# Block diagonal by small DMAs, column-tiled state weights, merged row sums and a new order of steps in a one-core kernel

## The chip, the cores and the metric

One core of one Trainium2 chip. The metric is device microseconds of one execution. Most executions of a kernel agree within a few tenths of a per cent here, but some are slower: a run is called slow when it is over 1.5% above the fastest of the same kernel. Verdicts use the other runs, called fast, and each kernel is compared with runs of the kernel before made in the same rounds on the same chip. A ratio below is the mean time of a kernel's fast runs over the mean of the fast runs of the kernel before of the same rounds, so it is not quite the ratio of the medians that are quoted. Intervals are 95%.

TensorE is PE in the profile, its weight loads are PEld, VectorE is DVE, ScalarE is ACT, GpSimd is POOL. Times in the views are microseconds from the start of the span. The span is about 1.8 us shorter than the run's time.

## The reference, cut to what matters

```python
# x: 8 batches x 8 heads x 512 x 64, state: 8 x 8 x 32 x 64
a  = softmax(scale * x @ state.T)        # 512 x 32 a head
xread = a @ state
a2 = softmax(scale * state @ x.T)        # 32 x 512
sread = a2 @ x
y = concat([xread, sread], axis=2)       # 8 x 8 x 544 x 64
# heads put side by side: z is 8 x 544 x 512
wq, wk = z @ w_q, z @ w_k                # 544 x 64
W = wq @ wk.T / 8
out = maximum(W @ z, 0) @ w_out          # 8 x 544 x 512, float32
```

Of the kernel before, what the change touches and what calls it, by code (L numbers as in the profile page):

```python
# [8 lines left out]
FP = mybir.dt.float32  # L9
# [4 lines left out]


ORDER = """
zst.0.p ix1.0.p stc.0.v xc1.0.a fill.1.t stt.0.c ste.0.v stbd.0.p stf.0.a xc0.0.p xc3.0.v ix2.0.p
fill.7.t xT0.0.t xc2.0.v xTe0.0.a fill.1.t xT1.0.t is.0.p stc.1.v fill.1.t stt.1.c xTe1.0.v stbd.2.p
fill.1.t pt0.0.t stf.1.v fill.1.t pt1.0.t exp0.0.a ste.1.v iwo.0.p exp1.0.a rs0.0.v fill.4.t
sums.0.t ix3.0.p rinv0.0.v wc.0.a fill.1.t xT0.1.t rs1.0.v fill.1.t srd.0.r xTe0.1.v A0.0.p fill.1.t  # L20
xT1.1.t fill.1.t sw.0.r xTe1.1.a rinv1.0.v fill.1.t pt0.1.t srn.0.v A1.0.p at0.0.t srT.0.t exp0.1.a
pt1.1.t srTe.0.v sbd.0.p swe.0.a xT0.2.t rs0.1.v at1.0.t exp1.1.a xT1.2.t xTe0.2.v stbd.1.p ate.0.a
xTe1.2.v fill.1.t stt.2.c stt.3.c rs1.1.v ste.2.a pt0.2.t stbd.6.p stf.3.v exp0.2.a fill.1.t wq.0.c
ste.3.v wks.0.c ix4.0.p stf.2.a wk.0.t rs0.2.v sw.3.r pt1.2.t wke.0.v swe.3.a stbd.3.p sw.1.r
rinv.1.v exp1.2.a g.0.t sw.2.r ge.0.v stbd.5.p swe.1.a rs1.2.v sums.2.t v.0.c wqe.0.a rinv.2.v
xT1.3.c swe.2.a A.1.p ve.0.v xT0.3.c xTe1.3.a srd.2.r xTe0.3.v mix0.0.r mix1.0.r mxe0.0.v sums.1.t
mxe1.0.a A.2.p srd.1.r at.1.t pt1.3.t srn.1.v ate.1.a fin0.0.t srn.2.v ix5.0.p xT1.4.t exp1.3.a
srT.1.t xT0.4.t xTe1.4.v srTe.1.a fin1.0.t sbd.1.p xTe0.4.a rs1.3.v pt1.4.t wq.1.c sbd.2.p exp1.4.a
wks.1.c wqe.1.v pt0.4.t oe0.0.a srT.2.t wk.1.t rs1.4.v at.2.t ix6.0.p fin2.0.t ate.2.v wke.1.a
os0.0.s exp0.4.a stbd.7.p g.1.t srTe.2.v fin3.0.t ge.1.v rs0.4.v sums.4.t stbd.4.p oe1.0.a srd.4.r  # L30
rinv.4.v v.1.c srn.4.v wq.2.c A.4.p ve.1.a os1.0.s srT.4.c wks.2.c wk.2.t srTe.4.a mixs.1.r wke.2.v
mix1.1.r wqe.2.a mix0.1.r mse.1.v xT1.5.t mxe0.1.a ix7.0.p at.4.t xTe1.5.v g.2.t xT0.5.t mxe1.1.a
ge.2.v sbd.4.p pt1.5.t xTe0.5.v v.2.c exp1.5.a fin2.1.c ve.2.v pt0.5.c rs1.5.v mixs.2.r mix1.2.r
exp0.5.a ate.4.v xT1.6.c mse.2.a sums.5.c fin3.1.c xTe1.6.a rs0.5.v rinv.5.v xT0.6.c mxe1.2.a
oe1.1.v A.5.p pt1.6.c wq.4.c srd.5.r exp1.6.a mix0.2.r srn.5.v os1.1.s fin0.1.c mxe0.2.a rs1.6.v
sbd.5.p xT0.7.c xTe0.6.v fin0.2.c xTe0.7.a wqe.4.v pt0.6.c srT.5.c at.5.c exp0.6.a xT1.7.c ate.5.v
srTe.5.a fin1.2.c xTe1.7.a rs0.6.v wq.5.c rinv.6.v wks.5.c wk.5.c wqe.5.a pt1.7.c A.6.p wke.5.v
wks.4.c sums.6.c exp1.7.a srd.6.r g.5.t oe0.2.a rs1.7.v wk.4.t pt0.3.t fin1.1.t srn.6.v exp0.3.a
os0.2.s wke.4.v sbd.6.p at.6.t oe0.1.a rs0.3.v srT.6.t g.4.t fin2.2.t ate.6.v os0.1.s fin3.2.t
ge.5.v ge.4.v srTe.6.v v.5.c oe1.2.a rinv.3.v wq.6.c ve.5.v A.3.p wks.6.c wk.6.c v.4.c os1.2.s  # L40
wke.6.a wqe.6.v mix1.5.r ve.4.a mixs.5.r mix0.5.r mxe1.5.v sums.3.t mxe0.5.a g.6.t srd.3.r mixs.4.r
ge.6.v mix0.4.r mse.5.a mix1.4.r srn.3.v mxe0.4.a v.6.c mse.4.v sbd.3.p srT.3.c pt0.7.c srTe.3.v
at.3.c mxe1.4.a ve.6.v fin2.5.c ate.3.v exp0.7.a fin3.5.c rs0.7.v wq.3.c oe1.5.a wks.3.c fin0.4.c
rinv.7.v A.7.p wqe.3.a os1.5.s mix0.6.r mixs.6.r wk.3.t mse.6.a fin1.4.t wke.3.a mxe0.6.a g.3.t
oe0.4.v at.7.t sums.7.t ate.7.a srd.7.r mix1.6.r srn.7.v os0.4.s fin2.4.c mxe1.6.v sbd.7.p srT.7.c
fin3.4.c srTe.7.a ge.3.v fin2.6.c oe1.4.v v.3.c fin3.6.c ve.3.v os1.4.s fin0.5.c oe1.6.a fin1.5.c
os1.6.s mix1.3.r oe0.5.v mixs.3.r wq.7.c mxe1.3.a wks.7.c wk.7.c mixs.0.r mse.3.v mix0.3.r os0.5.s
mse.0.a wke.7.v fin0.6.c wqe.7.a mxe0.3.a g.7.c fin1.6.c ge.7.a fin0.3.c oe0.6.v fin1.3.c os0.6.s
v.7.c oe0.3.a fin2.3.c ve.7.a fin3.3.c os0.3.s mix0.7.r oe1.3.a mixs.7.r fs.3.t mxe0.7.v mse.7.a
os1.3.s mix1.7.r fse.3.v fs.7.t mxe1.7.a fse.7.v fix1.7.t fix2.7.t oc1.7.a fix0.7.t oc2.7.a fix3.7.t  # L50
oc0.7.a oc3.7.b
"""


# [1 line left out]
def kernel(  # L56
# [9 lines left out]
    nc = tc.nc  # L66
    ctx.enter_context(tc.manual_schedule())

    B, H, S, D = x.shape
    NS = state.shape[2]  # L70
# [6 lines left out]
    NP = H // 2  # L77
# [13 lines left out]
    st_bf = const.tile([128, B, 2, D], BF, name="st_bf")  # L91
    stT = const.tile([128, B, 2, H, NS], BF, name="stT")
    stbd = const.tile([128, B, 2, NP, D], BF, name="stbd")
    w_f = const.tile([128, NP, 2, DH], FP, name="w_f")
    w_qk = const.tile([128, NP, 2, DH], BF, name="w_qk")
    w_o = const.tile([128, KC, DM], BF, name="w_o")
    sw = const.tile([128, B, 2, 2, DH], BF, name="sw")
# [35 lines left out]
    nc.vector.memset(mask, 0.0)  # L133
    for q in range(NP):
        nc.vector.memset(mask[NS * q : NS * q + NS, q : q + 1], 1.0)

    L = [dict() for _ in range(B)]
    G = {}
# [59 lines left out]
        copy(e, st_bf[:, b0:b1], st_f[:, b0:b1])  # L198

    def zeros(n, b, e):  # L200
        nc.gpsimd.memset(stT.bitcast(FP), 0.0)

    def w_cast(n, b, e):
        if e == "p":
# [36 lines left out]
    def sw_mm(n, p, e):  # L241
        ps = psA.tile([128, 2, 512], FP, name="sw_ps", tag="psA")
        for bb in range(2):
            for q in range(NP):
                for r in range(2):
                    nc.tensor.matmul(
                        out=ps[NS * q : NS * q + NS, r, 2 * DH * bb : 2 * DH * bb + 2 * DH],
                        lhsT=stT[64 * r : 64 * r + 64, 2 * p + bb, r, NP * r + q, :],
                        rhs=w_qk[64 * r : 64 * r + 64, q, 0:2, :],
                        start=True,  # L250
                        stop=True,
                    )
        G["sw", p] = ps
# [363 lines left out]
    def fs_ev(n, b, e):  # L617
# [5 lines left out]
    STEP = {  # L623
        "ix": load, "iwo": load, "is": load, "wc": w_cast, "xc": x_cast, "stc": st_cast,
        "zst": zeros, "stt": st_tr, "ste": st_ev, "stf": st_ev,
        "stbd": stbd_blk, "fill": fill, "fix": fin_mm, "os": fin_st,
        "sw": sw_mm, "swe": sw_ev, "xT": xT_mm, "xTe": xT_ev, "xs": x_dT, "as": a_dT, "pt": pt_mm, "exp": pt_exp,
        "rs": rs, "rinv": rv, "A": nrm, "at": at_mm, "ate": at_ev,
        "srd": srd, "sums": sums, "srn": srn, "sbd": sbd, "srT": srT_mm, "srTe": srT_ev,
# [5 lines left out]
    for tok in ORDER.split():  # L635
        n, b, e = tok.split(".")
# [31 lines left out]
```

## The kernel before: the parts that the change and the argument touch

The kernel is written as a list of steps, `name.batch.engine`. Every engine runs its own steps in the order of this list, so the list is the schedule. For PE the last letter is the form of a matmul: `t` is one 128x128 tile, `c` is two column halves (two instructions), `r` is a form of its own (row or 32-column tiles). `ix` and `iwo` are loads of x and of the output weights, `stbd` the block diagonal of the state, `sw` the state times the projection weights, `rs` row sums, `fill` matmuls on zeros that only keep PE running.

```python
ORDER = """
zst.0.p ix1.0.p stc.0.v xc1.0.a fill.1.t stt.0.c ste.0.v stbd.0.p stf.0.a xc0.0.p xc3.0.v ix2.0.p
fill.7.t xT0.0.t xc2.0.v xTe0.0.a fill.1.t xT1.0.t is.0.p ... iwo.0.p exp1.0.a rs0.0.v fill.4.t
sums.0.t ix3.0.p ...
"""                                        # cut; some 400 steps

def load(n, b, e):
    if n == "iwo":
        nc.gpsimd.dma_start(out=w_o, in_=moe_w_out.rearrange("(k p) e -> p k e", p=128))
    elif n == "is":
        nc.gpsimd.dma_start(out=st_bf[:, 3:B], in_=st_src[:, 6 : 2 * B])
    else:
        b = int(n[2:])
        nc.gpsimd.dma_start(out=x_bf[b], in_=xsrc(b, 0, H))       # 512 KB of x, cast on the way

def zeros(n, b, e):
    nc.gpsimd.memset(stT.bitcast(FP), 0.0)

def stbd_blk(n, b, e):                     # one batch: two multiplications on GpSimd
    for r in range(2):
        nc.gpsimd.tensor_tensor(out=stbd[:, b, r], in0=st_bf[:, b, r : r + 1, :].to_broadcast((128, NP, D)),
            in1=mask[:, :, None].to_broadcast((128, NP, D)), op=ALU.mult)

def sw_mm(n, p, e):                        # 16 matmuls for two batches
    for bb in range(2):
        for q in range(NP):
            for r in range(2):
                nc.tensor.matmul(
                    out=ps[NS * q : NS * q + NS, r, 2 * DH * bb : 2 * DH * bb + 2 * DH],
                    lhsT=stT[64 * r : 64 * r + 64, 2 * p + bb, r, NP * r + q, :],
                    rhs=w_qk[64 * r : 64 * r + 64, q, 0:2, :], start=True, stop=True)

for tok in ORDER.split():
    n, b, e = tok.split(".")
    STEP["".join(i for i in n if not i.isdigit())](n, int(b), e)
```

The softmax here doesn't subtract the row's maximum and nothing guards it: scores larger than these inputs give would overflow.

## Time and profile before

| | before |
|---|---|
| time, median of the runs beside the changed kernel | 88.25 us (87.77 to 88.51, 4 runs) |
| span of the profiled run | 87.0 us |
| PE busy | 80.8 us, 93% |
| DVE, ACT, POOL busy | 52.4, 55.9, 45.1 us |
| PE idle inside the span (87.0 - 80.8) | 6.2 us |
| instructions of PE and PEld in the trace | 1572 + 1579 |

The table is read from the top: one engine is busy 93% of the span, no other above 64%, so the length of PE's stream sets the time. The lines behind it stand in the prediction. The last row also belongs here, and the prediction did not look at it.

One more view of the kernel before belongs here: the posts of x on GpSimd, from its timeline (start, duration, engine, line, operation). This one is batch 4.

```profile
17.71 0.94 POOL L183 DMA_DIRECT2D x_bf<-in_x_dram  x1
```

### The profile page before, as it was taken

The page shows a single profiled execution, that of the slowest core. Times are in us where ns is not written, and L with a number is a line of the kernel's source. Part 1 is how long each engine was busy: PE and PEld are TensorE (multiplying, and loading weights), DVE is VectorE, ACT ScalarE, POOL GpSimd, SP SyncE. Part 2 cuts the span into 40 slices and gives each one's busy share as a digit, 9 for nine tenths or more (in the row PEclk, how much of TensorE's full clock was granted, in tenths as well). Part 3 has the DMA queues.
Part 4 walks back from the last instruction along what each step waited for, and adds up shares of the span by engine and source line. Part 5 has one row for each costly group of instructions (what it writes and reads, how often), then busy time and mean ns, then how long its engine had stood idle before and what let it go on. Part 6 is the DMA issues. An engine that isn't in the chain of part 4 may idle for free.

```text
span 87.0 us, 3553 instructions
## 1 busy us (share of the span) xinstructions
PE 80.8 (93%) x1572; PEld 53.4 (61%) x1579; DVE 52.4 (60%) x111; ACT 55.9 (64%) x83; POOL 45.1 (52%) x58
## 2 busy tenths in 40 slices
PE   4999999999999999999999999999999999999910
PEld 1326666878777778777689747866755565544400
DVE  2125793997956875897856957891688264056010
ACT  1541637999898858778797838967930592665530
POOL 7999948999999969408507735327150000000000
PEclk9999999999999999999999999999999999999996
DMA  0899999999609999995600464201461663566782
GB/s 12 292 312 187 202 191 198 195 165 147 96 0 121 143 128 277 322 169 72 241 8 4 171 281 175 115 8 53 188 243 45 275 281 136 213 269 277 294 314 80
DMA packets 15119, 15.00 MB, mean 172 GB/s; under 512 B 3712, under 2 KB 12672, under 8 KB 15104
## 3 DMA queue, kind: packets, MB, share of 16 engines
q0 software_dynamic: 9104, 4.36, 39.7%
q1 hardware_dynamic: 4880, 8.98, 28.0%
q10 hardware_dynamic: 1120, 1.44, 4.6%
q8 instruction: 12, 0.20, 0.9%
q14 instruction: 3, 0.02, 0.1%
HBM read 10.22 MB, written 8.91 MB: 220 GB/s over the span
## 4 chain that ended last, share of the span: by engine, by line
PE 90%; ACT 4%; issue 1%; DVE 1%
PE fin_ps L161 20%; PE fin_ps L163 12%; PE fill_ps L155 6%; PE xT_ps L174 5%; PE mix_ps L541 5%; PE warm_ps L132 4%; PE srd_ps L369 3%; PE xT_ps L170 3%; PE at_ps L174 3%; PE v_ps L505 3%; PE pt_ps L163 2%; PE g_ps L163 2%; PE fins_ps L163 2%; PE wq_ps L433 2%; PE v_ps L514 2%; PE wk_ps L163 2%
## 5 line engine op out<-in xcount | busy, mean ns | idle before, releaser
L346 POOL TENSOR_TENSOR A<-E,rinv 128x1024 bf16<-128x1024 bf16 (+1 forms) x9 | 15.4, 1717 | 12.8 <-DVE rinv L340 12.5
L161 PE MATMUL fin_ps<-w_o,rmix 128*64 128x512 bf16 x160 | 19.4, 380 | 0.0
L142 ACT COPY ost<-fin_ps 128x1024 f32<-128x1024 f32 (+2 forms) x13 | 11.2, 864 | 11.6 <-PE fin_ps L161 5.9
L148 ACT ACTIVATE rmix<-mix_ps 128x1024 bf16<-128x1024 f32 x12 | 12.1, 1024 | 2.4 <-PE mix_ps L541 2.4
L407 POOL TENSOR_TENSOR sbd<-srn,mask 128x256 bf16<-128x256 bf16 x16 | 9.4, 614 | 6.0 <-DVE srn L397 5.9
L144 DVE COPY ost<-fin_ps 128x1024 f32<-128x1024 f32 (+1 forms) x6 | 6.5, 1091 | 9.9 <-PE fin_ps L163 5.4
L161 PEld LDWEIGHTS <-rmix 128*64 128x64 bf16 x160 | 8.4, 110 | 6.2 <-issue 0.6
L332 DVE TENSOR_REDUCE rsum<-E 128x16 f32<-128x512 bf16 x16 | 10.8, 676 | 0.9 <-ACT E L317 0.6
L163 PE MATMUL fin_ps<-w_o,rmix 128*128 128x512 bf16 x44 | 11.0, 379 | 0.2
L317 ACT ACTIVATE E<-pt_ps 128x512 bf16<-128x512 f32 x16 | 9.5, 601 | 2.5 <-PE pt_ps L161 1.3
L142 ACT COPY xT<-xT_ps 128x1024 bf16<-128x1024 bf16 x7 | 7.1, 1012 | 4.6 <-PE xT_ps L174 3.9
L234 POOL TENSOR_TENSOR stbd<-st_bf,mask 128x256 bf16<-128x256 bf16 x16 | 9.3, 610 | 0.4 <-DVE st_bf L144 0.2
L155 PE MATMUL fill_ps<-zero 128*128 128x512 bf16 x21 | 7.8, 432 | 0.1
L144 DVE COPY xT<-xT_ps 128x1024 bf16<-128x1024 bf16 x9 | 6.2, 690 | 2.7 <-PE xT_ps L174 2.5
L150 DVE TENSOR_SCALAR rmix<-mix_ps 128x1024 bf16<-128x1024 f32 x4 | 4.9, 1222 | 3.4 <-PE mix_ps L541 3.4
L163 PEld LDWEIGHTS <-rmix 128*128 128x128 bf16 x48 | 4.3, 98 | 4.0 <-ACT rmix L148 0.2
L183 POOL DMA_DIRECT2D x_bf<-in_x_dram x7 | 6.6, 949 | 0.0
L174 PE MATMUL xT_ps<-ident,x_bf 128*128 128x128 bf16 x80 | 6.0, 219 | 0.2 <-ACT E L317 0.2
L174 PEld LDWEIGHTS <-x_bf 128*128 128x128 bf16 x80 | 5.1, 98 | 1.3 <-issue 0.5
L541 PE MATMUL mix_ps<-wq,V 64*128 64x256 bf16 x64 | 5.8, 272 | 0.0
L132 PE MATMUL warm_ps<-zero 128*128 128x512 bf16 x8 | 3.6, 631 | 1.2 <-DVE mask L133 1.2
L163 PE MATMUL pt_ps<-stT,xT 128*128 128x64 bf16 x88 | 4.4, 193 | 0.0
(90 smaller groups left out, 139.7 us busy)
## 6 DMA issues: line engine op xcount, KB each, us to landing
out_dram<-ost SPq DMA_DIRECT2D x14, 512.0 KB, 2.8
x_bf<-in_x_dram POOLq DMA_DIRECT2D x7, 512.0 KB, 7.8
out_dram<-ost ACTq DMA_DIRECT2D x3, 256.0 KB, 2.1
x_f<-in_x_dram ACTq DMA_DIRECT2D x2, 256.0 KB, 4.0
x_f<-in_x_dram SPq DMA_DIRECT2D x2, 256.0 KB, 4.4
w_o<-in_moe_w_out_dram POOLq DMA_DIRECT2D x1, 512.0 KB, 8.4
out_dram<-ost SPq DMA_DIRECT2D x2, 256.0 KB, 2.4
st_bf<-in_state_dram POOLq DMA_DIRECT2D x1, 160.0 KB, 7.8
```

Source lines behind the costliest of these rows:

```text
L142: nc.scalar.copy(out=out, in_=in_)
L144: nc.vector.tensor_copy(out=out, in_=in_)
L148: nc.scalar.activation(out=out, in_=in_, func=AF.Relu)
L155: nc.tensor.matmul(out=ps, lhsT=zero[:, 0:128], rhs=zero, start=True, stop=True)
L161: nc.tensor.matmul(out=out[64 * h : 64 * h + 64], lhsT=lh, rhs=rhs, **kw)
L163: nc.tensor.matmul(out=out, lhsT=lhsT, rhs=rhs, **kw)
L174: nc.tensor.transpose(out=out, in_=in_, identity=ident)
L317: nc.scalar.activation(out=L[b]["E"][:, r].rearrange("p c q n -> p c (q n)"), in_=L[b][f"pt{r}"], func=AF.Exp, scale=float(scale),)
L332: nc.vector.reduce_sum(out=L[b]["rsum"][:, w], in_=L[b]["E"].rearrange("p r c q n -> p (r c q) n")[:, w], axis=AX.X,)
L346: eng.tensor_tensor(out=L[b]["A"].rearrange("p r c q n -> p (r c q) n")[:, w], in0=L[b]["E"].rearrange("p r c q n -> p (r c q) n")[:, w], ...
L407: nc.gpsimd.tensor_tensor(out=L[b]["sbd"][:, r], in0=L[b]["srn"][:, r : r + 1, :].to_broadcast((128, NP, D)), in1=mask[:, :, None].to_broa ...
L541: nc.tensor.matmul(out=ps[:, h, kk, :], lhsT=L[b]["V"][rows, 128 * k : 128 * k + 128], rhs=L[b]["wq"][rows, 0:SH], start=True, stop=True,)
```

## The change

The intent: fewer changes of PE's tile shape (each 0.11 us), less GpSimd work, fewer fillers, x of batch 3 in time. The list of steps is rewritten throughout; the diff is cut to its head and to the code.

```diff
 ORDER = """
-zst.0.p ix1.0.p stc.0.v xc1.0.a fill.1.t stt.0.c ste.0.v stbd.0.p stf.0.a xc0.0.p xc3.0.v ix2.0.p
-fill.7.t xT0.0.t xc2.0.v xTe0.0.a fill.1.t xT1.0.t is.0.p ... iwo.0.p exp1.0.a rs0.0.v fill.4.t
-sums.0.t ix3.0.p rinv0.0.v ...
+zst.0.p ix1.0.p stc.0.v fill.1.t stt.0.c stbd.0.p ste.0.a stf.0.v xc1.0.a xc0.0.p xc3.0.v ix2.0.p
+fill.5.t xT0.0.t xc2.0.v fill.1.t xT1.0.t xTe0.0.v is.0.p xTe1.0.v fill.1.t pt0.0.t ix3.0.p exp0.0.a
+stc.1.v fill.1.t pt1.0.t sbs.0.s fill.1.t stt.1.c exp1.0.a iwo.0.p rs0.0.v stf.1.a rinv0.0.v
 ... (cut: all 36 lines of the list are new; rs0.b and rs1.b become rs.b for batches 3 to 7)
@@
+    nc.vector.memset(stT.bitcast(FP), 0.0)
@@
     def zeros(n, b, e):
-        nc.gpsimd.memset(stT.bitcast(FP), 0.0)
+        nc.gpsimd.memset(stbd[:, 1:B].bitcast(FP), 0.0)
+
+    def stbd_put(n, g, e):
+        b0, b1 = ((1, 3), (3, B))[g]
+        for q in range(NP):
+            rows = slice(NS * q, NS * q + NS)
+            nc.sync.dma_start(out=stbd[rows, b0:b1, :, q, :], in_=st_bf[rows, b0:b1])
@@ sw_mm
-                        lhsT=stT[64 * r : 64 * r + 64, 2 * p + bb, r, NP * r + q, :],
-                        rhs=w_qk[64 * r : 64 * r + 64, q, 0:2, :],
+                        lhsT=stT[:, 2 * p + bb, r, NP * r + q, :],
+                        rhs=w_qk[:, q, 0:2, :],
```

## The prediction

> **What bounds the kernel now.** I read the busy table and the slices first, then the chain of waits, then the chain in order of time, then the groups by form and the DMA issues.
>
> ```profile
> PE 80.8 (93%) x1572; PEld 53.4 (61%) x1579; DVE 52.4 (60%) x111; ACT 55.9 (64%) x83; POOL 45.1 (52%) x58
> PE   4999999999999999999999999999999999999910
> PE 90%; ACT 4%; issue 1%; DVE 1%
> ```
>
> TensorE (PE) is busy in every slice from the second to the 38th, and 90% of the chain that ended last is PE's own instructions. VectorE (DVE), ScalarE (ACT) and GpSimd (POOL) sit near 50 to 64%. So the time is the length of PE's instruction stream, with few holes. What matters is what each piece of it costs; the chain in order of time tells that.
>
> ```profile
> 31.28 0.18 PE srd_ps L163 x8
> 31.46 0.35 PE srd_ps L369 x32
> 31.81 0.34 PE v_ps L505 x2
> ...
> 52.73 0.25 PE wk_ps L161 x16
> 52.98 0.22 PE v_ps L505 x2
> ```
>
> The same two instructions (V, line 505) take 0.34 us after the 32-column tiles of line 369 and 0.22 us after matmuls in their own 128x64 tile shape. The difference, 0.11 us, is a change of tile shape.
>
> ```profile
> 18.93 0.34 PE wk_ps L163 x8
> 19.27 0.24 PE sw_ps L246 x16
> 19.51 0.34 PE pt_ps L163 x8
> 19.84 0.24 PE sw_ps L246 x16
> 20.08 0.34 PE g_ps L163 x8
> ...
> 27.42 0.23 PE pt_ps L163 x8
> ```
>
> Eight pt matmuls take 0.23 us undisturbed and 0.34 beside a block of sw (the state weights), so a lone sw block costs 0.24 + 0.11 us, of which 0.13 is its own work and 2 x 0.11 the two changes of shape.
>
> ```profile
> 5.57 2.29 PE fill_ps L155 x7
> 7.86 0.45 PE xT_ps L174 x8
> 8.31 0.22 PE fill_ps L155
> ...
> 13.63 1.01 ACT xT L142
> 14.65 0.60 ACT E L317
> ...
> 17.28 0.79 ACT stT L142
> 18.07 0.50 ACT E L317
> ```
>
> These are the fillers: matmuls on zeros that keep PE running while the first batch is on its way; 0.22 us each once the clock is up. The two ACT stretches, near 14 and 18 us, are the only true holes: PE waits there for an eviction.
>
> **What the skill says.** First, the Trainium skill, "TensorEngine Tiling (Array Packing)", Key Properties: changing the tiling mode, not just the tile, drains TensorE. The trace agrees, at 0.11 us a change. Second, "TensorE: Matmul & The Clock Gate", Part 3, The mechanism: matmuls keep program order in start and end; only different tiles overlap. The trace fits: 32 matmuls of line 369, whose column group changes every time, take 0.24 us beside the drain. No row of this profile has two in sequence on one column group. Third, "VectorE: DVE Perf Modes", Zero memsets can be issued as uint32: a memset takes one cycle per element. The trace has 256 elements in 272 ns (first line below). Fourth, "DMA: Bandwidth & Descriptors", Why small descriptors are slow (HBM only): copies inside SBUF escape the penalty of small descriptors; the run before has no such copy to check it with.
>
> ```profile
> L126 DVE MEMSET zero<- 128x256 uint32 x1 | 0.3, 272 | 0.9 <-PEq L652 0.9
> L201 POOL MEMSET stT<- 128x2048 f32 x1 | 1.8, 1804 | 0.0
> L234 POOL TENSOR_TENSOR stbd<-st_bf,mask 128x256 bf16<-128x256 bf16 x16 | 9.3, 610 | 0.4 <-DVE st_bf L144 0.2
> L332 DVE TENSOR_REDUCE rsum<-E 128x16 f32<-128x512 bf16 x16 | 10.8, 676 | 0.9 <-ACT E L317 0.6
> ```
>
> **Part by part.**
>
> Block diagonal by DMA: 14 of the 16 POOL multiplications go, 14 x 0.61 = 8.5 us, and the POOL memset of 2048 elements (1.80) becomes one of 1792 (1.58 by the same rate), so POOL falls from 45.1 to about 36.4. The memset of stT moves to DVE: 2048 elements at 272/256 ns are 2.2 us, between the mask at 1.6 and the first cast of the state, which started at 3.67 after waiting 2.1 for its load. It is hidden to within 0.2 us. The DMAs bring 512 + 1280 = 1792 rows of 128 bytes. At the 61 ns a packet of the POOL queue (39.7% of 16 x 87.0 us over 9104 packets), an estimate for this size, that is 6.8 us of all 16 engines, in an early phase when they are 90% busy. POOL and DMA are not the bound, so none of this shortens the time by itself.
>
> Row sums merged for batches 3 to 7: five instructions of 512 elements go. 676 ns is 533 of streaming and 0.14 fixed, so DVE saves 5 x 0.14 = 0.7 us. Off the path.
>
> State weights over the full 128 rows: still 64 matmuls, now in 128x32 tiles, the shape of srd. That removes row tiling, and three of the four blocks now stand next to an srd block or share its run. But the two halves r of one q fall on the same column group, one after the other. If only different groups overlap, 16 matmuls of 128 columns take about nine slots of 53 ns, 0.48 us a block; if all four groups fill perfectly, 0.22. Own work rises from 0.5 us to 0.9 to 1.9 us in all.
>
> New order. I listed PE's steps in both orders by tile shape and counted the changes. Before 58, after 41: 17 x 0.11 = 1.9 us saved. Eight of the removed changes are sw's; the rest are from mix, whose 12 separate runs in row tiles become 8, and from srd of batches 5 and 6 standing together. Fillers: 23 before, 19 after, two fewer ahead of the first xT: 4 x 0.22 = 0.9 us. All other PE steps are the same in number and cost; more of them are written as two column halves, which costs 0.02 us a block.
>
> Check of this sum on the kernel before, from the first xT at 7.86 to the last matmul's end at 82.92, 75.06 us: useful groups 63.3, 15 fillers 3.2, state transposes 0.8, sw 0.5, 56 changes 6.2, together 74.0; so 1.1 us of holes. After: 63.4 + 13 fillers 2.8 + 0.8 + sw 0.9 to 1.9 + 39 changes 4.3 = 72.2 to 73.2, and the head is 0.4 shorter. PE's end thus moves by 1.2 to 2.2 us if the holes stay; I take 1.7.
>
> The holes. I walked the head with the durations above: the first xT at 7.3, the second batch's transposes from 11.7, wq of batch 0 at 15.9 instead of 17.95, with 0.8 us less work done by then. That is 1.25 us gained, of which 0.85 is fillers, so after sw's extra cost 0.5 us of holes go. Its limit is x of batches 2 and 3: the POOL loads landed 7.8 us after issue in the median.
>
> ```profile
> x_bf<-in_x_dram POOLq DMA_DIRECT2D x7, 512.0 KB, 7.8
> w_o<-in_moe_w_out_dram POOLq DMA_DIRECT2D x1, 512.0 KB, 8.4
> ```
>
> Batch 2 landed at about 13.5 and is wanted at 14.3. Batch 3, ahead of the output weights now, should land near 17.2 to 18.2 instead of 19.9 and is wanted at 18.1. The output weights come some 2.5 us later than 17.5, wanted after 24.
>
> The end gives a little back: the three mix blocks of batch 7 stand together, and behind them the last output needs evictions of 0.44 and 1.02 to 1.22 us, which before had the fs block of batch 3 beside them. I charge 0.2, and 0.2 for new holes in the middle.
>
> Sum: -1.7 - 0.5 + 0.2 + 0.2 = -1.8 or -1.9 us, so 88.36 becomes about **86.5 us**, 2.1% less.
>
> **Rivals.** (a) The sw blocks serialise and eat the switching gain, and a few holes open: 0.7 to 1 us gained, 87.4. For it: the loop order, q outside r. Against: the block was put beside srd, which pays only if it is cheap enough. (b) The small DMAs and the reordered loads delay batch 3 or 4: PE waits 1 to 2 us near 18 or 25 us, and the time is 87.5 to 88.5. For it: DMA at 90% until 22 us. Against: the HBM loads of the POOL queue run far below the 320 GB/s of the early slices, so the copies may use gaps. (c) The order was tuned so that almost all the 1.1 us of holes go and sw costs 0.9: 85.5. (d) POOL's 8.5 us bring a gain of their own through earlier A and sbd blocks; the 90% of PE in the chain speaks against it.
>
> **Range and chances.** The sum runs from 1.2 to 2.9 gained before surprises, and the 2% line is 86.59, almost at my estimate. I take **85.5 to 87.7 us** as the range of 8 in 10, and **0.5 faster, 0.48 within 2%, 0.02 slower**.
>
> **What would show it.** The changed profile should have 19 fillers; mix runs whose drains are paid 8 times; the sw piece at 0.22 to 0.5 us, with none of 0.34 in its neighbours on either side as now; POOL near 36 us busy; wq of batch 0 near 16 us; the first xT near 7.3; PE ending near 81. I am wrong if the chain shows DMA waits for x, more than 1.5 us of ACT or DVE pieces inside it, or an sw piece above 0.5 us.

## The result, and the profile after

The changed kernel took 93.28 us in the median (92.22 to 95.12, 4 runs) against 88.25. The ratio of fast runs is 1.054 [1.043, 1.064]: slower. Its granted clock was 0.97 to 0.98.

The run that was profiled with it was the slow one of the four, 95.12 us; two of the three fast ones were granted 0.97 as well and were not profiled. Of its page, the busy line, PE's slices with the clock, and the shares of the chain that ended last:

```profile
PE 81.3 (87%) x1615; PEld 56.5 (61%) x1619; DVE 52.9 (57%) x103; ACT 55.5 (59%) x88; POOL 36.8 (39%) x44
PE   4998978999770999999999997999999999998910
PEclk9999999999998589999999999999999999999995
PE 71%; DMA 11%; issue 6%; DVE 4%; ACT 2%; POOL 2%; DVEq 0%
```

PE is busy about as long as before in a longer span. There is a dip in slices 11 to 13, and the clock falls to half right behind it. "issue", time in which PE waits for nothing that the profile shows, went from 1% to 6%. The chain in order of time (start, length, what) tells where:

```profile
5.76 10.15 DMA x_bf<-in_x_dram
...
23.70 0.62 issue
...
27.30 0.05 PE srd_ps L375 x7
27.36 2.89 issue
30.24 0.56 PE srd_ps L375 x25
30.81 1.82 PE xT_ps L174 x16
```

The first line is the "DMA 11%": x of batch 2, posted at 5.76 and landed at 15.91. PE stood 0.65 us for x of batch 1 and 0.29 us for this one. By the prediction's own sign, a DMA wait for x in the chain, it was wrong in this run there too; the second profile below has no such piece.

PE stops for 2.89 us in the middle of one step: 7 of the 32 matmuls of srd are done, and the other 25 have the same operands and wait for no other engine. No semaphore and no buffer can explain a stop at that place. Behind it the clock is down: 16 transposes take 1.82 us, where 16 took 0.92 to 1.00 us at full clock.

A second profile, of the same kernel in a single later run (experiment 1, 92.1 us, close to the fastest of the four; clock 0.988), is the better one to compare with. Its busy line, and the "issue" pieces of its chain:

```profile
PE 79.6 (88%) x1615; PEld 55.5 (61%) x1619; DVE 53.0 (59%) x103; ACT 55.3 (61%) x88; POOL 37.1 (41%) x44
```

```profile
17.06 0.27 issue
...
22.12 1.13 issue
...
26.29 2.07 issue
...
53.54 0.81 issue
```

PE's busy time fell by 1.2 us (80.8 to 79.6), about as predicted. Its idle time rose by 4.5 us, from 6.2 to 10.7 (90.3 - 79.6). The sum, 3.3 us, is the whole difference of the two spans. The four pieces are 4.28 us. In the kernel before no "issue" piece of the chain after the first 2 us is longer than 0.16 us.

**Where the holes stand.** I put PE's records (matmuls, weight loads and a few semaphore instructions) in order of their starts and counted. In the second profile the four holes stand before records 448, 704, 960 and 2238: the first three are exactly 192 + 256k, the last is two records before 2240, and some records can be missing from a trace. So these stops, which the profile explains by nothing, fall on every 256th instruction.

The missing records can be put back: the traces of experiments 13 and 14, with the same PE steps, have seven matmuls more than the kernel before and four more than the changed kernel. Then all four holes stand at 193 + 256k (449, 705, 961 and 2241), and so do the holes of every other profile here. I keep the names 448, 704, 960 and 2240 below. The DMA table of the page has a queue that fits:

```profile
q8 instruction: 12, 0.20, 0.9%
```

These are 12 transfers of 16 KB, 64 bytes for each of 256 instructions. The Trainium skill, "Runtime: NRT & Kernel Launch", Instruction fetch mechanics, says the same of the size: an engine's instructions come in 16 KiB blocks of 256, fetched by its sequencer while the block before is being run. It adds that the cost of crossing a block is "mostly hidden". The trace agrees on the block and not on the cost.

The transfers of that queue and the records of PE give this table. "Asked" is the start of the first instruction of a block, "fetch" is the start of the transfer of the block after it. That the next block is asked for at that moment is my reading: in these three profiles no fetch began before it, to within 0.01 us, and none later than 3.9 us after it. In some other profiles a few fetches late in the run began before it, by 2.0 us at most (experiments 11 and 15), so what exactly asks is not shown.

```
block        before                          changed, profiled         changed, second profile
from         asked  fetch          hole      asked  fetch       hole   asked  fetch       hole
192          12.46  15.22 (+2.76)  -         11.48  15.38 (+3.90)  -    10.96  14.81 (+3.85) 0.43
448          18.22  18.72 (+0.50)  -         18.76  22.03 (+3.27)  0.84 17.33  20.99 (+3.66) 1.35
704          22.15  22.71 (+0.56)  -         24.32  27.81 (+3.49)  3.08 23.25  26.00 (+2.75) 2.26
960          27.32  27.38 (+0.06)  -         30.24  31.35 (+1.11)  -    28.35  29.72 (+1.37) -
(hole: time between the starts of the last record of that block and the first of the next,
 so some 0.2 us longer than the piece of the chain)
```

The transfer itself takes 0.9 us, and in the five holes of the table PE goes on 1.4 to 1.6 us after it has landed (landed at 28.76, on at 30.24 in the long one). Over all 17 profiles there are 35 such holes, and PE goes on 1.2 to 1.6 us after the landing in each; nowhere does it start a block sooner than 1.2 us after the block landed. So a block that runs for less than the delay and some 2.3 us more leaves a hole. In the kernel before, the blocks from 448, 704 and 960 ran 3.9, 5.2 and 5.3 us, and the fetches of their successors began 0.06 to 0.56 us after the ask. In the changed kernel the block from 704 was done in 2.84 us, and the fetch of its successor began only 3.49 us after the ask: the new order puts two sw, two srd, sums, wq, wks and wk side by side there, nearly all short instructions.

The DMA view of two windows of the changed kernel (queue: packets, MB, share of 16 engines) shows what the fetch came behind. From 20 to 22 us:

```profile
q0 software_dynamic: 663, 0.35, 131.0%
q1 hardware_dynamic: 250, 0.03, 19.8%
```

From 22 to 24 us:

```profile
q1 hardware_dynamic: 1049, 0.13, 47.6%
q0 software_dynamic: 161, 0.08, 28.4%
q8 instruction: 1, 0.02, 2.7%
```

q0 is GpSimd's queue (x and the output weights), q1 here carries the small DMAs of the block diagonal; shares go over 100% because the times of packets overlap. The block asked for at 18.76 moves at 22.03, when q0 has thinned out.

The rest of the profile is as intended or nearly: GpSimd 36.8 us busy, and an sw block next to srd in 0.26 us. From the chain of the second profile:

```profile
24.47 0.26 PE sw_ps L252 x16
```

### The profile page after: what moved, and what is told of

Same layout as the page of the kernel before. It is cut to its first block, busy times and chain, and to the rows that moved or that the text cites. A ratio compares the mean times of both kernels' runs of the same rounds, so it can differ in the third digit from the quotient of the medians.

```text
span 93.3 us, 3625 instructions
## 1 busy us (share of the span) xinstructions
PE 81.3 (87%) x1615; PEld 56.5 (61%) x1619; DVE 52.9 (57%) x103; ACT 55.5 (59%) x88; POOL 36.8 (39%) x44
## 4 chain that ended last, share of the span: by engine, by line
PE 71%; DMA 11%; issue 6%; DVE 4%; ACT 2%; POOL 2%; DVEq 0%
PE fin_ps L161 21%; DMA x_bf<-in_x_dram 11%; PE fin_ps L163 10%; PE xT_ps L174 5%; PE mix_ps L547 4%; PE srd_ps L375 3%; PE v_ps L511 2%; PE at_ps L170 2%; PE wq_ps L439 2%; PE pt_ps L161 2%; PE pt_ps L163 2%; PE xT_ps L170 2%; DVE stT L135 2%; PE v_ps L520 2%; PE wk_ps L163 2%
## 5 line engine op out<-in xcount | busy, mean ns | idle before, releaser
L352 POOL TENSOR_TENSOR A<-E,rinv 128x1024 bf16<-128x1024 bf16 (+1 forms) x9 | 15.4, 1714 | 18.6 <-ACT E L323 10.5
L161 PE MATMUL fin_ps<-w_o,rmix 128*64 128x512 bf16 x176 | 20.9, 379 | 0.2 <-ACT rmix_s L148 0.2
L413 POOL TENSOR_TENSOR sbd<-srn,mask 128x256 bf16<-128x256 bf16 x16 | 9.4, 609 | 13.8 <-PE mix_ps L547 6.8
L161 PEld LDWEIGHTS <-rmix 128*64 128x64 bf16 x176 | 11.1, 110 | 5.7 <-issue 0.2
L338 DVE TENSOR_REDUCE rsum<-E 128x16 f32<-128x512 bf16 (+1 forms) x11 | 10.0, 916 | 0.1
L174 PE MATMUL xT_ps<-ident,x_bf 128*128 128x128 bf16 x96 | 7.9, 235 | 1.3 <-DMA x_bf<-in_x_dram 1.0
L144 DVE COPY xT<-xT_ps 128x1024 bf16<-128x1024 bf16 x11 | 7.6, 691 | 2.1 <-PE xT_ps L174 1.3
L142 ACT COPY xT<-xT_ps 128x1024 bf16<-128x1024 bf16 x5 | 5.1, 1036 | 6.1 <-PE xT_ps L174 6.1
L174 PEld LDWEIGHTS <-x_bf 128*128 128x128 bf16 x96 | 6.4, 106 | 2.8 <-DMA x_bf<-in_x_dram 1.4
L144 DVE COPY AT<-at_ps 128x1024 bf16<-128x1024 bf16 x6 | 4.1, 690 | 4.0 <-PE at_ps L174 2.3
L375 PE MATMUL srd_ps<-x_bf,E 128*32 128x64 bf16 x256 | 3.6, 200 | 2.9 <-issue 2.9
L375 PEld LDWEIGHTS <-E 128*32 128x32 bf16 x256 | 2.6, 99 | 3.5 <-issue 3.2
## 6 DMA issues: line engine op xcount, KB each, us to landing
st_bf<-in_state_dram POOLq DMA_DIRECT2D x1, 160.0 KB, 10.7
```

Source lines behind the costliest of these rows:

```text
L142: nc.scalar.copy(out=out, in_=in_)
L144: nc.vector.tensor_copy(out=out, in_=in_)
L161: nc.tensor.matmul(out=out[64 * h : 64 * h + 64], lhsT=lh, rhs=rhs, **kw)
L174: nc.tensor.transpose(out=out, in_=in_, identity=ident)
L338: nc.vector.reduce_sum(out=L[b]["rsum"][:, w], in_=L[b]["E"].rearrange("p r c q n -> p (r c q) n")[:, w], axis=AX.X,)
L352: eng.tensor_tensor(out=L[b]["A"].rearrange("p r c q n -> p (r c q) n")[:, w], in0=L[b]["E"].rearrange("p r c q n -> p (r c q) n")[:, w], ...
```

## The experiments

Two theories at the start. **S**: PE stops for its own instructions, because blocks are fetched late and used up quickly. **D**: the small DMAs and the exchanged loads delay data (x, block diagonal), and the stops are waits that the profile fails to name.

### 1. after_again: the changed kernel once more

No edit.

> The changed kernel once more, for one look. Theory S (supply): PE stands still where its own instruction stream crosses a multiple of 256, because the 16 KB block of instructions was fetched late; the profile before this run has a hole of 2.9 us inside the srd block of batch 3, one of 0.6 us inside at of batch 1 and one of 0.6 us inside pt of batch 7, each at such a multiple. S expects the same holes at the same matmuls, perhaps of other size, and 91 to 95 us. Theory D (small DMAs delay the loads of x): expects x of batches 1 and 2 to land 9 to 10.5 us after issue again. If both were accidents of one run, the holes and the late landings are gone here and the span is under 90.5 us.

92.1 us. Holes at the three instructions of the first profile (before 704, 960 and 2238; there 0.84, 3.08 and 0.80 us) with other lengths, 1.35, 2.26 and 1.00 us, and a fourth of 0.43 us before 448. A fixed place in the instruction stream with a changing length speaks for S. The landing of x was 7.8 us after issue in the median, as before the change, so the 9.6 of the first profile is not general.

### 2. after_pool_diag: the block diagonal on GpSimd again

```diff
-... sbs.0.s ... sbs.1.s ...
+... sbd.0.p stbd.1.p ... sbd.1.p stbd.2.p ... (one stbd.b.p for each batch 1 to 7)
```

> The changed kernel with the block diagonal of batches 1 to 7 built by GpSimd again, no small DMA; all else as changed. D: x of batches 1 and 2 land within 8 us of issue again, PE's waits on DMA near 12 and 15.5 us go, and the time falls to 87 to 89. S with the small copies as the only cause of late instruction blocks: the hole at srd of batch 3 goes too, 86.5 to 88.5. S with the order as the cause (too many small matmuls in a row while x loads): holes stay, 91 to 94. Rival P: GpSimd, with 8.5 us more to do, delays A and sbd and the loads behind them, and the time stays above 91 with waits on POOL in the chain.

92.04 us (91.12 to 92.46), ratio 1.040 [1.030, 1.049]. Without a single small DMA it is still 4% behind. Holes of 1.35, 0.59, 1.37 and 1.07 us remain, at 704, 960, 1472 and 2240 (the last in part a wait for DVE). No wait for GpSimd stands in the chain, so rival P is not the reason. The small DMAs are not the main cause; the difference from 1.054 says that they may add a per cent or so, but the intervals overlap.

### 3. before_small_dma: the small DMAs alone, in the kernel before

```diff
+    nc.vector.memset(stT.bitcast(FP), 0.0)
-        nc.gpsimd.memset(stT.bitcast(FP), 0.0)
+        nc.gpsimd.memset(stbd[:, 1:B].bitcast(FP), 0.0)
+    def stbd_put ... (as in the change)
-... stbd.2.p ... stbd.1.p ... stbd.7.p stbd.4.p ...
+... sbs.0.s ... sbs.1.s ...
```

> The kernel before with the small DMAs alone (and the memset of stT on VectorE that goes with them). D: x lands later and the time grows by 1 to 3 us, 89 to 91.5. S with the copies as the cause: at least one hole of over 0.5 us at a multiple of 256 of PE's instructions, 89 to 92. If the order is the cause of it all: 87.5 to 88.8, as before.

91.38 us (90.27 to 92.69, two of the four runs fast), ratio 1.034 [1.022, 1.045]. From its chain:

```profile
8.46 12.74 DMA x_bf<-in_x_dram
...
22.26 1.27 issue
```

x of batch 3 landed 12.7 us after issue (10.0 in the kernel before) and now stands in the chain; and there is a hole of 1.27 us, again at the end of a block. The block after 448 came 3.60 us after the ask, not 0.50. So this part alone costs 3%. But GpSimd, with less to do, also posted x of batch 4 at 14.7 instead of 17.7 us. Both theories can claim this run; experiment 13 separates them.

### 4. after_ix5_late: x of batch 5 posted later

```diff
-srd.2.r exp1.3.a sw.2.r ix5.0.p srn.2.v
+srd.2.r exp1.3.a sw.2.r srn.2.v ... sbd.3.p ix5.0.p exp0.4.a
```

> The changed kernel with only the load of x of batch 5 issued later, behind sbd of batch 3 instead of ahead of srn of batch 2. In the profile its packets ran from 24 to 27.9 us, and the block of PE instructions that PE stood waiting for started only when they ended. S with DMA traffic as what delays the block: the hole at srd of batch 3 shrinks from 2.9 to under 1 us, and the time falls by 1 to 3 us. If the block comes late for another reason, or the hole is not a matter of instructions: the hole stays at 2 to 3 us. The load may be late for batch 5 itself; then PE waits on DMA ahead of its transposes near 37 us.

96.37 us (95.38 to 96.64), ratio 1.088 [1.079, 1.097]: slower, where S had hoped for faster. The hole at 960 is indeed gone, and the block from 960 came 1.05 us after the ask instead of 2.8 to 3.5. But the load itself came too late, and the clock fell to 0.95:

```profile
30.42 6.74 DMA x_bf<-in_x_dram
```

A miss on the time, a hit on the hole: the moment of posting a load of x changes when the next instructions arrive.

### 5. after_split2: the loads of x and of the output weights in halves

```diff
-            nc.gpsimd.dma_start(out=x_bf[b], in_=xsrc(b, 0, H))
+            k = H // [1, 1, 2, 2, 2, 2, 2, 2][b]
+            for h0 in range(0, H, k):
+                nc.gpsimd.dma_start(out=x_bf[b][:, h0 : h0 + k], in_=xsrc(b, h0, h0 + k))
```

> The changed kernel with each GpSimd load of x of batches 2 to 7 and of the output weights cut into two DMAs of half the size, same bytes. Theory S2: PE's next block of 256 instructions waits behind the share of one load that lies on its DMA engine; a load of 1024 rows puts 64 rows of 60 ns there, 3.84 us, and the longest delays seen in four profiles are 3.66 to 3.90 us. With halves no delay should pass about 2 us, so the holes at PE instruction 704 and 960 shrink from 1.35 and 2.3 us to under 0.7 together, and the time falls by 2 to 3.5 us, to 88.5 to 90.5. Rival: the delay is general DMA load, not the size of one load; then delays of 3 us or more stay, and so does the time, 91 to 93. GpSimd spends about 0.8 us more on each issue, which may cost up to 1 us near 11 us.

92.78 us (92.37 to 94.86), ratio 1.048 [1.036, 1.059]. Holes 1.35, 2.26 and 0.73 us, delays still up to 4.2 us. The idea that the delay is the size of one posted load falls.

### 6. after_split4: x of batches 4 to 7 in quarters

```diff
-            k = H // [1, 1, 2, 2, 2, 2, 2, 2][b]
+            k = H // [1, 1, 2, 2, 4, 4, 4, 4][b]
```

> As the last, but x of batches 4 to 7 in four DMAs of a quarter each. S2: delays of blocks asked for while these load fall to 1 us or so; the hole at 960 is gone; 88 to 90. Rival general load: no difference from the changed kernel. If GpSimd's issue time bites (3.2 us a batch instead of 0.95), it is slower than the halves, with POOL in the chain.

91.19 and 90.38 us in the two fast runs, 92.04 and 93.42 in the slow ones; too few for a ratio. The hole at 960 is gone, those at 704 (1.58 us), 1472 (0.48) and 2240 (1.04) are not. Quarters also take longer to post, so this moves the posts as well as the sizes, and settles nothing alone.

### 7. after_six_fills: more PE work ahead of the long hole

```diff
-wqe.1.a srT.2.t sums.3.t
+wqe.1.a srT.2.t fill.6.t sums.3.t
```

> The changed kernel with six more filler matmuls, 6 x 0.216 = 1.3 us of PE work, put ahead of the row sums of batch 3, in the stretch of 256 instructions that ends with the largest hole. S: PE has to wait for the next block anyway, so the fillers fall into the hole and the time stays within 0.4 us of the changed kernel's 92 (the hole shrinks by about 1.3). If PE's own stream were the bound there: 1.3 us more.

91.78 us (91.4 to 92.3), ratio 1.038 [1.028, 1.048]. Six fillers, 1.3 us of useless work on the engine that bounds the kernel, cost nothing: it is if anything faster than the changed kernel, and its clock stayed at 0.999 to 1.0. The chain shows the hole behind them shortened, from 2.07 to:

```profile
27.69 1.22 issue
```

PE is waiting there for something that comes when it comes, whatever PE does before. With the holes' places this is what S says.

### 8. before_sw_cols: column-tiled state weights alone

The two lines of `sw_mm` as in the change, nothing else.

> The kernel before with the state weights over 128 rows alone. The prediction's sum: 4 blocks, 8 changes of shape stay in this order, so 0 to 0.25 us more for each block, 88.4 to 89.4. In the changed kernel a block took 0.25 us beside srd, which says four column groups do overlap: then at most 0.4 us more, and no hole of its own.

88.97 us (88.41 to 89.16), ratio 1.005 [0.996, 1.015]: same. In the old order none of the four sw blocks has a neighbour of its shape. Three of them stand where PE has no other wait; each is 0.35 us in the chain, where it was 0.24 in the kernel before:

```profile
20.23 0.35 PE sw_ps L246 x16
```

Three times 0.11 us is 0.4% of the time, which agrees with the ratio and cannot be told from none. The 0.26 us of the changed kernel come from the new neighbours.

### 9. after_order_only: the new order without small DMAs and without the exchange of loads

```diff
-pt0.0.t ix3.0.p exp0.0.a ... sbs.0.s ... exp1.0.a iwo.0.p rs0.0.v ... sbs.1.s
+pt0.0.t iwo.0.p exp0.0.a ... exp1.0.a ix3.0.p rs0.0.v ... (and stbd.b.p as in 2)
```

> The changed kernel with the block diagonal by GpSimd and the output weights loaded ahead of batch 3 again, as before; what stays of the change is the order, the column-tiled state weights and the merged row sums. Supply theory: the order is enough to run PE into late instruction blocks, holes of over 0.5 us at PE instruction 704 or 960 remain, 90 to 92.5. If loads and small copies were the whole cause: 86.5 to 88.5 and no such hole.

97.09 us in the median; one fast run of 94.08, three slow ones up to 99.08, clock 0.93 to 0.98; no ratio. Two lines of its chain:

```profile
8.43 12.18 DMA x_bf<-in_x_dram
...
40.24 2.28 issue
```

The new order wants x of batch 3 by about 17.5 us, and behind the output weights it lands at 20.6. So the exchange of loads belongs to the order, and of the whole change the order is the part that cannot stand alone. The wait for x stands at record 555, in the middle of a block, and the profile names what it waits for; the holes for instructions stand at 960, 1472 and 2240 (0.70, 2.28 and 0.41 us in the chain), and it names nothing.

### 10. before_x3_first: the exchange of loads alone

```diff
-exp0.0.a ste.1.v iwo.0.p exp1.0.a rs0.0.v fill.4.t sums.0.t ix3.0.p
+exp0.0.a ste.1.v ix3.0.p exp1.0.a rs0.0.v fill.4.t sums.0.t iwo.0.p
```

> The kernel before with only the loads of batch 3 and of the output weights exchanged. The first use of batch 3 lies near 21 us and of the output weights near 24.7, so the exchange by itself should change nothing: 88.0 to 89.2. If the exchange delays the instruction block fetched near 18.7 us to near 21, as in the changed kernel, a hole of 0.5 to 1.5 us opens at instruction 704 and the time is 89 to 90.5.

88.25 us (87.99 to 89.59), ratio 1.002 [0.998, 1.007]: same. x of batch 3 landed at 17.7, as the prediction had said of the changed kernel; the old order has no use for it that early.

### 11. after_thin: fewer instructions where the last hole stood

```diff
-A.6.p at.5.c sums.5.c oe0.2.a pt1.7.c ... srT.5.c at.6.c ... pt0.7.c
+A.6.p at.5.t sums.5.t oe0.2.a pt1.7.t ... srT.5.t at.6.t ... pt0.7.t
```

Six steps between 51 and 57 us as one 128-wide matmul instead of two column halves: 82 fewer PE instructions, two more shape changes.

> The changed kernel with six blocks near 51 to 57 us (transposes of A of batches 5 and 6, row sums of 5, pt of 7 and the transpose of srn of 5) in one matmul of 128 columns in place of two of 64: same work, 82 PE instructions fewer, and two changes of shape more, 0.22 us. Supply theory: the hole near 54 us, 0.8 to 1.1 us at PE instruction 2240 in every profile of this order, closes to under 0.3, the holes at 704 and 960 stay, and the time falls by 0.3 to 0.9 us. If the hole is something else it stays, and the time grows by 0.2.

92.73 us (91.22 to 93.16), ratio 1.044 [1.037, 1.051]. The hole at 2240 is gone, and no "issue" piece above 0.2 us is left in its chain but the two near 22 (1.25 us) and 26 us (2.07). Two things changed there: the block from 1984 ran for 2.8 us (2.4 in the second profile, without its hole), and the next one came 0.1 us after the ask (1.1). Which of them closed the hole is not separated. The gain in time is not shown either: the interval overlaps that of the changed kernel.

### 12. before_fewer_fills: four fillers fewer

```diff
-ix2.0.p fill.7.t xT0.0.t ... rs0.0.v fill.4.t sums.0.t
+ix2.0.p fill.5.t xT0.0.t ... rs0.0.v fill.2.t sums.0.t
```

> The kernel before with four fillers fewer, at the same two places as in the change (7 to 5 and 4 to 2). The prediction's sum gives 0.9 us. Supply theory: PE instruction 448 can't start before the block fetched near 15 us is usable, near 17.3 us in all profiles, and is at 18.2 in the kernel before, so at most 0.9 us can be had up to there: 87.5 to 88.5 for 88.5 before. If a hole opens instead: no change.

87.91 us (87.71 to 89.29), ratio 0.999 [0.996, 1.002]: same. The prediction counted 0.9 us for these four. In this run's chain the head is a load:

```profile
9.93 11.15 DMA x_bf<-in_x_dram
```

PE was some 0.7 us ahead of the kernel before at 18.6 us; then it waited for x of batch 3, which landed at 21.08 (19.95 in the kernel before), and at its end it was 0.24 us ahead. So most of what the fillers gave up was lost again behind a load.

What was open by then: whether the time of posting sets the late fetch, in the kernel before too, and whether a changed kernel without these holes gains. Three more runs were for that.

### 13. before_x4_early: in the kernel before, x of batch 4 posted earlier

```diff
-sbd.0.p swe.0.a ... wq.0.c ste.3.v wks.0.c ix4.0.p stf.2.a
+sbd.0.p ix4.0.p swe.0.a ... wq.0.c ste.3.v wks.0.c stf.2.a
```

> The kernel before with the load of x of batch 4 posted some 2 us earlier, near 15.5 us in place of 17.7, so ahead of the moment when PE reaches instruction 448 and asks for its next block (17.6 to 18.2 us); nothing else. Posting theory: that block, fetched 0.5 us after it was asked for in the kernel before, now starts 2 to 3.5 us after, a hole of 0.5 to 1.5 us opens at instruction 704, and an earlier load makes the kernel slower, 88.6 to 90. Rival, general DMA traffic (the engines are busy until 22 us in either case): fetch delay and time as before, 87.6 to 88.5.

91.2 us (89.94 to 91.73, two of the four runs fast), ratio 1.026 [1.018, 1.034], more than expected. By the 2% line the verdict is unclear; that it is slower is clear. The profiled run is a slow one (91.73), in which the clock fell to half for 3.4 us behind the hole; that adds to its time. The clock fell only at 24.1 us, after the hole, so it is not what made the hole. The two fast runs were not profiled. The post of this load in GpSimd's timeline, to set beside the line of the kernel before, and the new hole in the chain:

```profile
15.48 0.94 POOL L183 DMA_DIRECT2D x_bf<-in_x_dram  x1
```

```profile
22.42 1.61 issue
```

PE's work, its order and its operands are those of the kernel before. One load is posted 2.2 us earlier, the block after 448 comes 3.31 us after the ask instead of 0.50, and PE stops for 1.61 us at the end of a block. PE goes on at 24.03, 1.55 us after that block has landed (22.48). This is the clearest of the runs. It also weakens D's claim to experiment 3: the earlier post, which the small DMAs bring about by freeing GpSimd, makes such a hole with no small DMA there.

### 14. after_posted_late: in the changed kernel, x of batches 4 and 5 held back

```diff
+    def x_hold(n, b, e):
+        nc.vector.memset(x_bf[b][:, 0, 0:1], 0.0)     # the load must come after it
-... g.0.t ix4.0.p pt0.2.t ...
+... wqe.0.a pt1.2.t rs0.1.v xh.4.v ix4.0.p ... ate.1.v xh.5.v srd.2.r ... ix5.0.p
```

> The changed kernel with x of batch 4 held back until VectorE has done the row sums of batch 1, and x of batch 5 until it has evicted the transposes of A of batch 1; both then post just after PE has asked for a block. Posting theory: the blocks start within 1.5 us of being asked for (2.7 to 3.7 before), the holes at 704 and 960 shrink from 3.6 together to under 1, and the time falls by 1.5 to 3 us, to 89 to 90.5. Rival general traffic: holes stay, 91 to 93. The loads come later; a wait on DMA ahead of batch 4 or 5 would show in the chain.

89.36 us (89.04 to 89.81), ratio 1.013 [1.009, 1.018], the same at 2%: three quarters of the loss gone (1.054 to 1.013). The posts moved from 13.8 and 21.1 us (second profile of the changed kernel) to 17.6 and 24.2. The "issue" pieces of the chain above 0.2 us are 0.27, 0.67, 0.42 and 0.40 us, 1.76 in all instead of 4.28; the one at 704 was 1.13:

```profile
22.07 0.67 issue
```

One half of the expectation missed: the fetch of the block after 448 still began 3.20 us after its ask (3.66 in the second profile), not within 1.5: asked for at 17.08, begun at 20.28, where it had been 17.33 and 20.99. The fetch after that came 1.07 us after its ask, where it had been 2.75.

### 15. after_best: 14 with the thinned steps of 11 and the end in the old order

```diff
 (14 and 11, and)
-fs.3.c oe0.5.a mixs.7.r mix1.7.r fse.3.a mse.7.v mix0.7.r
+oe0.5.a mix0.7.r os0.5.s mixs.7.r fs.3.t mxe0.7.v mse.7.a mix1.7.r fse.3.v
```

> after_posted_late with the thinned blocks near 54 us and with the end's order as before (the output of batch 3's state rows between the two mix blocks of batch 7). 0.3 to 0.9 and 0.3 to 0.5 us less than after_posted_late: 88 to 89.5. It may tie with the kernel before; that it beats it clearly is not expected.

88.8 us (88.5 to 90.02), ratio 1.006 [1.002, 1.010]: within 2%, and just behind the kernel before. Two holes of 0.59 and 0.44 us are left in its chain. PE is busy 79.3 us, 1.5 less than in the kernel before, but idle 7.4 us (span 86.7) instead of 6.2. No version ran clearly ahead of the kernel before.

## Why the prediction was wrong

It said 86.5 us, range 85.5 to 87.7, with 2% for slower. It is 93.3, and 92.1 in the run of the second profile, to which the sizes below refer.

**What held.** PE's stream is the bound, before and after. A change of shape costs what it did (wq's four matmuls 0.34 us behind one, 0.22 without). GpSimd came to 36.8 us (36.4 predicted). sw beside srd took 0.26 us, near the 0.22 of four filled column groups and not the 0.48 of nine slots, so rival (a) falls. x of batch 3 landed at 18.1 us in the second profile (issued at 7.79, 10.3 us later); 17.2 to 18.2 were predicted, and wq of batch 0 began at 15.84 (15.9).

**Right by luck.** PE's busy time fell by 1.2 us, the low end of the 1.2 to 2.2 of the sum, but from the fillers alone. Their lines, before and in the second profile:

```profile
L155 PE MATMUL fill_ps<-zero 128*128 128x512 bf16 x21 | 7.8, 432 | 0.1
L155 PE MATMUL fill_ps<-zero 128*128 128x512 bf16 x18 | 6.8, 415 | 0.0
```

In the profiles of experiments 10 (old order) and 14 (new order), from which no PE record is missing, they have 5.7 and 4.6 us of PE's busy time, each instant counted once, and all the rest has 74.9 and 74.8. The changes of shape are 58 and 41 in these traces too, as the prediction counted; but the 17 x 0.11 us saved, less the 0.3 us that sw became dearer, do not show in PE's busy time. Where they went was not traced.

**The step that failed: "The holes."** It walked the head by the waits for data and evictions, found that "0.5 us of holes go", and charged "0.2 for new holes in the middle". The sum had no term for the supply of PE's own instructions. That term measured 4.3 us in the chain. It has two causes in the change. The order packs the short instructions, so a block of 256 lasts 2.8 us where three in a row had lasted 3.9 to 5.3. And x of batch 4 is posted earlier (13.8 or 16.2 us instead of 17.7), after which the next block came 3.3 to 3.7 us after its ask instead of 0.5. Experiments 7, 11, 13 and 14 show both sides: work put into the hole is free, a thinned block loses its hole (with the fetch sooner too), an earlier post makes one in the old order, a later post takes most of the loss away in the new one.

**"POOL and DMA are not the bound, so none of this shortens the time by itself."** True, and only half of the matter: freeing GpSimd made it post loads earlier. The small DMAs alone, with the earlier posts that follow from them, cost 3.4% in the kernel before.

**"4 x 0.22 = 0.9 us" of fillers.** Measured by itself it is nothing (0.999, experiment 12).

**"I charge 0.2" for the end.** The chain of the second profile has 0.46 us of wait for the eviction of rmix_s near the end and 0.27 us of "issue" behind it, 0.7 us, and another 0.47 us for such an eviction at 70.5 us. The lines of the end:

```profile
80.77 0.46 DVE rmix_s L150
81.23 0.27 issue
```

With the old order at the end (experiment 15) the one at 80.8 is gone.

**The rivals.** Rival (b), DMA traffic that makes PE wait near 18 or 25 us, named about the right places and the right kind of cause, but for x, and at 87.5 to 88.5 us. It is PE's instructions that come late there.

**Smaller terms.** The memset of stT took 1.76 us, not 2.2, because the 272 ns for 256 elements hold a fixed part: one element takes 59 ns, so the others take 0.84 ns each, which gives 1.77 for 2048. A merged row sum took 1.21 us against 2 x 0.67, so 0.13 saved, as charged. The "320 GB/s of the early slices" is a misreading; they show 292 and 312.

The account nearly closes on the two profiled runs, 88.75 and 92.1 us. PE's busy time fell by 1.2 us where the sum had 1.7, and its idle time rose by 4.5 where the sum had it fall by 0.1 (-0.5 + 0.2 + 0.2). That is 5.1 of the 5.6 us between 92.1 and 86.5. Another 0.4 is that the prediction started from 88.36. The slow run of 95.12 us adds the waits for x and the lowered clock that followed its hole of 2.89 us.

**What stays open.** Why a block waits. A wait for the loads posted before the ask fits most cases (in experiment 13 the fetch came at 21.58, the load landed at 22.62). But in the kernel before a block came 0.50 us after its ask while x of batch 3 was under way until 19.9, in experiment 10 one came 1.0 us after its ask while the output weights were under way until 20.2, and in experiment 14 one waited 3.20 us although x of batch 4 was posted only after its ask. That an earlier post makes it late is shown by 13; by what rule the transfers are served is not. Nor was it tried to take all of the delay away.

## What to carry to other kernels

Where PE is full of short instructions, count them in blocks of 256, the size seen here: a block that is run before the next one has come, while large loads are under way (blocks of 2.4 to 5.9 us did so in the changed kernel), can leave PE standing with nothing to wait for in the profile but "issue", in the middle of a step. A stream can then be made shorter in work and longer in time; check a new order for its densest blocks and for when the loads are posted, and not only for its data. An engine that is off the critical path still sets when loads are posted, so making it faster is a change of the traffic.

## What the Trainium skill lacked or had wrong

- "Runtime: NRT & Kernel Launch", Instruction fetch mechanics: it calls the cost of crossing a block mostly hidden, and gives PE room for 2048 instructions (a note in the same section says only two blocks, 32 KiB, which fits the trace better). Here PE stood up to 2.9 us at a block's end (4.3 us in one run of 92.1), and a block's transfer began 0 to 3.9 us after PE had started on the block before it (three profiles; up to 2.0 us earlier in experiments 11 and 15), so in those three PE never had more than one block in hand beyond the one it ran. No page gives a delay of this fetch behind loads that GpSimd posts (0.50 to 3.31 us when one load was posted 2.2 us earlier); how queues take turns on a DMA engine is told only in general.
- "DMA: Bandwidth & Descriptors", Why small descriptors are slow: it exempts copies inside SBUF but gives no time for one row. Here 128-byte rows between SBUF tiles took 14.5 ns each of one DMA engine between 22 and 24 us (47.6% of 16 x 2 us over 1049) and 25 ns between 20 and 22 us (19.8% over 250), against 63 ns for the rows of some 500 bytes of the GpSimd queue (131.0% over 663). That agrees with the page; the prediction's estimate of 61 ns was too high.
- No page says how long PE needs after a block of its instructions has landed: 1.2 to 1.6 us in the 35 holes of this case.
